# A dense layer over token groups of 512 instead of 384, with its weight remainders taken by VectorE

## The chip, the core and the metric

The kernel runs on one core of a Trainium2 chip. The metric is the device time of one execution in microseconds (us). Engines: TensorE (PE; its weight loads are shown apart as PEld), VectorE (DVE), ScalarE (ACT), GpSimd (POOL), and the queue of SyncE (SP), which here issues nearly all transfers.

## What is computed

Three stages follow each other. First, attention for 2 batches of 8 heads, 768 positions and 64 dimensions; a query sees only the keys whose six random sign bits equal its own. Second, a dense layer over the 1536 tokens with fp32 accuracy; third, a layer of eight experts in which each token goes through the expert with the largest gate logit:

```python
h = x @ w_in                      # 1536 x 512 by 512 x 2048
r = np.maximum(h, 0.0)
x2 = (s * (r * r) + b) @ w_out    # 2048 x 512
logits = x2 @ w_gate              # eight experts
e_idx = np.argmax(logits, axis=1)
# per token: gate_w * sigmoid(x2 @ w_output_gate[:, e]) * (relu(x2 @ w1[e]) @ w2[e])
```

Every large product is made of three in a rounded format: a value is split into a rounded part and its remainder, and high x high, high x low and low x high are added up.

## The kernel before, in words

The order of the work on every engine is the order of the program (a manual schedule); engines wait for each other through semaphores only.

**Attention** runs in 107 calls of `tick` (L230), one tile of 128 queries each. Every sixth tick ends one head pair's half of a batch: 384 tokens are copied to `xs` (L273), GpSimd rounds them to `xh` (L274), and VectorE takes the remainder `xl` in the next tick (L278). These are the dense layer's input, in four groups of 384 tokens, so that each half fills one group (L270). Ticks 84 to 95 are interleaved with the first three weight conversions (`convs`, L1021), and ticks 96 to 106 with the first dense steps.

**The dense layer** (`moe1`, L914) has 64 steps, 16 blocks of 128 hidden units for each of 4 groups, and two more that drain. Step s issues, in this order: the load of a later weight block (`stage`, L328, only in group 0, SP's queue, into five `stg` buffers), `mm1` of step s (L358: 12 matmuls of 384 columns into one PSUM bank, L368), the elementwise work of step s - 1, and `mm2` of step s - 2 (L394: for each of three token tiles three matmuls of 512 columns, L406 to L408). The elementwise work for s < 14 is four ScalarE operations (Relu L375, Square L379, scale and bias L380, rounding L381 to `gh`) and one on VectorE, the remainder `gl` (L390); from step 14 on, ScalarE L375, VectorE L383, ScalarE L384, VectorE L392. `r`, `gh` and `gl` have two buffers each.

**The weight conversion** (`conv`, L340) in steps 0 to 12 prepares block s + 3, once, in group 0: the weights arrive as 64 bit numbers, and VectorE puts the 32 bit ones together with three integer operations for each of two halves (L347, L349, L353). ScalarE rounds each half (L354), and GpSimd takes the remainder (L355):

```python
for k in range(2):
    nc.vector.scalar_tensor_tensor(m[k], t[k][:, :, 0], 29, m[k], ...)      # L353
    nc.scalar.copy(w[:, k, 0, :], m[k].bitcast(F32))                        # L354
    nc.gpsimd.tensor_tensor(w[:, k, 1, :], m[k].bitcast(F32), ...)          # L355
    yield
```

VectorE's order in such a step is: 2 x L347, 2 x L349, 2 x L353, then `gl` of the step before. The converted block of step s is first read by `mm1` three steps later.

**The gates** (`gate`, L410) follow each group: the three result tiles `y` are copied to `x2` (L416, ScalarE but for one), transposed on TensorE (`flip`, L429), multiplied with the gate weights (`logits`, L422), and VectorE finds each token's expert and weight in a row of small operations; then `x2` is stored to DRAM (L498). A gate is a generator: it is advanced once per step, and three times per step from step 50 on, after `mm1`, after the elementwise work and after `mm2`. `x2` and the transposed tiles share the five `stg` buffers. After the third gate `route_early` (L522) picks two experts with at least 128 tokens among those gated so far, loads their weights into the buffers of weight blocks that are done (L595) and gathers 128 tokens for each (L606), so that the first two of twelve expert passes can run while the last gate and `route` (L610) work. `mark` (L517) writes the table `am`, and `route` allots a table `pb` (L657), both in `stg` buffers.

**The expert layer** (`moe2`, L822) runs twelve passes of 128 tokens: per pass four weight segments, each split into two tiles by ScalarE (L752) and VectorE (L754), 12 matmuls per segment, and transposes of the hidden tile (`th`, L770) into three rotating `ht` buffers, two of which lie where the last group's `xh` and `xl` were. More passes follow only if the counts need them (`extra`, L883).

Of the kernel before, what the change touches and what calls it, by code (L numbers as in the profile page):

```python
# [20 lines left out]
NP = H // 2  # L21
# [5 lines left out]
XW = 513  # L27
NKEEP, NCONST = 222, 840
# [8 lines left out]
class Kernel:  # L37
# [5 lines left out]
    def consts(self, pool):  # L43
# [13 lines left out]
        self.cw = bf("cwb", 128)  # L57
# [172 lines left out]
    def tick(self, t):  # L230
# [35 lines left out]
        if t >= 15 and (t - 15) % 6 == 0:  # L266
            u = (t - 15) // 6
            n, half = divmod(u, 2)
            b, p = divmod(n, NP)
            g = 2 * b + half  # L270
            xp = st["xp"].pop(u)
            xs = self.xs_p.tile([128, HS], F32, name="xs")
            nc.scalar.copy(xs, xp)  # L273
            nc.gpsimd.tensor_scalar(self.xh[g][:, p, :], xs, 1.0, 1.0, ALU.mult, ALU.mult)  # L274
            st["xl"] = (self.xl[g][:, p, :], xs, self.xh[g][:, p, :].bitcast(F32))
        elif "xl" in st:
            o, i0, i1 = st.pop("xl")
            nc.vector.tensor_tensor(o, i0, i1, ALU.subtract)  # L278
# [61 lines left out]
    def conv(self, j):  # L340
# [11 lines left out]
        for k in range(2):  # L352
            nc.vector.scalar_tensor_tensor(m[k], t[k][:, :, 0], 29, m[k], ALU.logical_shift_right, ALU.bitwise_or)  # L353
            nc.scalar.copy(w[:, k, 0, :], m[k].bitcast(F32))  # L354
            nc.gpsimd.tensor_tensor(w[:, k, 1, :], m[k].bitcast(F32), w[:, k, 0, :].bitcast(F32), ALU.subtract)  # L355
            yield

    def mm1(self, s):  # L358
# [5 lines left out]
        h = self.ps1.tile([128, HS], F32, tag=tag, name="h", bufs=2 if tag == "tp" else 1)  # L364
# [7 lines left out]
    def elem(self, s):  # L372
        nc = self.nc
        r = self.g_p.tile([128, HS], F32, name="r", bufs=2)
        nc.scalar.activation(r, self.h.pop(s), AF.Relu)  # L375
        gh = self.g_p.tile([128, HS], F32R, name="gh", bufs=2)
        gl = self.g_p.tile([128, HS], F32R, name="gl", bufs=2)
# [16 lines left out]
    def mm2(self, s):  # L394
# [6 lines left out]
        for tt in range(3):  # L401
# [8 lines left out]
    def gate(self, g):  # L410
        nc, v = self.nc, self.nc.vector
        last = g == 3
        xts = []
        for tt in range(3):
# [4 lines left out]
        lts = self.cv_p.tile([128, 3, 128], F32, tag="cvm", name="lts", bufs=4)  # L419
        xt = []  # L420

        def logits(ts):  # L422
            lt = self.ps1.tile([128, 3, 128], F32, tag="tp", name="lt", bufs=2)
# [5 lines left out]
        def flip(tt):  # L429
            bank = ("pv", 1) if last and tt == 2 else ("tp", 2)  # L430
# [5 lines left out]
            else:  # L436
                if tt == 0:
                    self.t3 = self.x3_p.tile([128, 3, 4, 128], F32, tag="xl3", name="xt3")
                t = self.t3[:, tt]
            (nc.scalar.copy if last and tt == 1 else v.tensor_copy)(t, tp)  # L440
            xt.append(t)

        if last:
            for tt in range(3):
                flip(tt)
            yield
            logits([0, 1, 2])
# [5 lines left out]
        lp = self.ps1.tile([128, 3, 2 * E], F32, tag="tp", name="lp", bufs=2)  # L453
        for tt in range(3):
            nc.tensor.matmul(lp[:, tt, :], lts[:, tt, :], self.sel, start=True, stop=True)
        lg = self.small("lg", 3, 2 * E)
# [3 lines left out]
        bc = lambda a, k: a.unsqueeze(2).to_broadcast([128, 3, k])  # L460
        mx = self.small("mx", 3)
        v.tensor_reduce(mx, lg[:, :, 0:E], AX.X, ALU.max)
        df = self.small("df", 3, E)
        v.tensor_tensor(df, lg[:, :, 0:E], bc(mx, E), ALU.subtract)
        ex = self.small("ex", 3, E)
# [3 lines left out]
        wv = self.small("wv", 3, E)  # L469
        desc = self.c[:, 188:196].unsqueeze(1).to_broadcast([128, 3, E])  # L470
        v.scalar_tensor_tensor(wv, df, 0.0, desc, ALU.is_equal, ALU.mult)
        mw = self.small("mw", 3)
        v.tensor_reduce(mw, wv, AX.X, ALU.max)
        oh = self.oh[:, 3 * g:3 * g + 3, 0:E]
        v.tensor_tensor(oh, wv, bc(mw, E), ALU.is_equal)
        if not last:
            for k in range(3 * g, 3 * g + 3):
                v.tensor_tensor(self.cum[:, k + 1, :], self.cum[:, k, :], self.oh[:, k, 0:E], ALU.add)
            yield
        po = self.small("df", 3, E)  # L480
        v.tensor_tensor(po, oh, lg[:, :, E:2 * E], ALU.mult)
        ov = self.small("ov", 3)
        v.tensor_reduce(ov, po, AX.X, ALU.add)
        eo = self.small("eo", 3)
# [3 lines left out]
        se = self.small("se", 3)  # L488
# [3 lines left out]
        sc = self.small("sc", 3)  # L492
        v.reciprocal(sc, se)
        for tt in range(3):
            x2 = xts[tt]
            v.tensor_copy(x2[:, 512:513], sc[:, tt:tt + 1])
            k = 3 * g + tt
# [24 lines left out]
    def route_early(self):  # L522
        v, pe = self.nc.vector, self.nc.tensor
        nt = 9
        ps = self.ps1.tile([128, nt + 1, E], F32, tag="tp", name="rps", bufs=2)
        pe.matmul(ps, self.ones, self.hc.unsqueeze(2).to_broadcast([128, nt + 1, E]), start=True, stop=False)
        pe.matmul(ps, self.ones, self.cum, start=False, stop=False)
# [7 lines left out]
        for t in range(0, nt, 3):  # L535
            self.mark(t, t + 3, r[:, t:t + 3])
# [30 lines left out]
        pc = self.small("pe", 9, E)  # L567
# [29 lines left out]
        for P in range(2):  # L597
            self.gather(P, TOK - 384)
# [11 lines left out]
    def route(self):  # L610
        v, pe = self.nc.vector, self.nc.tensor
        oh = self.oh
        ps = self.ps1.tile([128, 4, E], F32, tag="tp", name="rps", bufs=2)
        pe.matmul(ps, self.ones, self.hc[:, 6:10].unsqueeze(2).to_broadcast([128, 4, E]), start=True, stop=False)
        pe.matmul(ps, self.ones, self.cum[:, 9:10, :].to_broadcast([128, 4, E]), start=False, stop=False)
        pe.matmul(ps[:, 0:3, :], self.tri, oh[:, 9:12, 0:E], start=False, stop=False)
        for t in range(3):
            pe.matmul(ps[:, t + 1:4, :], self.ones, oh[:, 9 + t:10 + t, 0:E].to_broadcast([128, 3 - t, E]), start=False, stop=(t == 2))
        n = ps[:, 3, :]
        sl = self.small("sl", E)  # L620
        v.tensor_scalar(sl, n, 1.0 / 128, MAGIC, ALU.mult, ALU.add)
        mr = self.small("pe", 9, E)[:, 0:3, :]
        v.tensor_tensor(mr, oh[:, 9:12, 0:E], ps[:, 0:3, :], ALU.mult)
        v.tensor_scalar(sl, sl, MAGIC, None, ALU.subtract)
        r = self.small("rr", 9)[:, 0:3]
# [3 lines left out]
        q = self.small("rq", 9)[:, 0:3]  # L629
# [9 lines left out]
        v.tensor_copy(oh[:, 9:12, E], q)  # L639
# [12 lines left out]
        self.mark(9, NT, r)  # L652
# [117 lines left out]
    def th(self, P, n):  # L770
# [5 lines left out]
        pool, tag = ((self.x3_p, "xh3"), (self.x3_p, "xl3"), (self.m2_p, "ht"))[self.nht % 3]  # L776
# [340 lines left out]
```

## Time and profile before

| | |
|---|---|
| median of 3 runs | 729.1 us (728.49 to 730.5) |
| profiled execution, its own time | 730.24 us |
| its span, first to last instruction | 728.5 us |
| TensorE busy | 687.6 us (94%) |
| VectorE busy | 490.1 us (67%) |
| ScalarE busy | 435.3 us (60%) |
| GpSimd busy | 242.8 us (33%) |
| mean granted TensorE clock | 0.984 of full speed |

Times in the rows are us from the span's start, durations us unless marked ns. A timeline row has start, duration, engine, line, operation, output <- inputs, shape, how many were merged, and in brackets the idle time of that engine just before with what ended it. Merged rows span from the first start to the last end. Consecutive matmuls overlap in the rows (one of L368 lasts 0.34 us, the next starts 0.18 later), so what one costs in a stream is the distance of the starts.

### The profile page before, as it was taken

The page shows a single profiled execution, that of the slowest core. Times are in us where ns is not written, and L with a number is a line of the kernel's source. Part 1 is how long each engine was busy: PE and PEld are TensorE (multiplying, and loading weights), DVE is VectorE, ACT ScalarE, POOL GpSimd, SP SyncE. Part 2 cuts the span into 40 slices and gives each one's busy share as a digit, 9 for nine tenths or more (in the row PEclk, how much of TensorE's full clock was granted, in tenths as well). Part 3 has the DMA queues.
Part 4 walks back from the last instruction along what each step waited for, and adds up shares of the span by engine and source line. Part 5 has one row for each costly group of instructions (what it writes and reads, how often), then busy time and mean ns, then how long its engine had stood idle before and what let it go on. Part 6 is the DMA issues. An engine that isn't in the chain of part 4 may idle for free. (4 is left out here: it accounts for less than half of the span.)

```text
span 728.5 us, 10938 instructions
## 1 busy us (share of the span) xinstructions
PE 687.6 (94%) x3888; PEld 537.1 (74%) x3888; DVE 490.1 (67%) x916; ACT 435.3 (60%) x802; POOL 242.8 (33%) x239
## 2 busy tenths in 40 slices
PE   6799999999998997779999999999999899999995
PEld 3566666666665666669889988988997668888873
DVE  4677768767779799992334233325557999898960
ACT  4788878878886574664222322232246599888850
POOL 4566667666667566450000000000100023212111
PEclk7899999999999999999999999999999999999999
DMA  9941352332503255500001000101660162111680
GB/s 207 230 88 66 87 146 72 87 110 55 199 1 105 70 190 215 173 30 1 0 1 45 1 1 0 44 1 41 237 258 1 49 244 98 44 45 44 213 315 28
DMA packets 17581, 69.94 MB, mean 96 GB/s; under 512 B 2990, under 2 KB 3886, under 8 KB 14064
## 3 DMA queue, kind: packets, MB, share of 16 engines
q1 hardware_dynamic: 15472, 62.61, 27.5%
q0 software_dynamic: 2048, 6.56, 2.7%
q8 instruction: 33, 0.54, 0.3%
q14 instruction: 28, 0.23, 0.1%
HBM read 100.61 MB, written 6.43 MB: 147 GB/s over the span
## 5 line engine op out<-in xcount | busy, mean ns | idle before, releaser
L368 PE MATMUL h<-xh,w 128*128 128x384 f32 x512 | 143.8, 341 | 0.0
L257 DVE TENSOR_REDUCE nm<-sp 128x1 f32<-128x768 f32 x96 | 91.4, 952 | 43.9 <-PE sp L255 41.9
L754 DVE TENSOR_TENSOR ring<-raw,ring 128x1024 fp32r<-128x1024 f32 x96 | 113.3, 1220 | 11.1 <-ACT ring L752 10.6
L308 POOL TENSOR_SCALAR pe<-pe,rd 128x768 f32<-128x768 f32 x96 | 90.5, 943 | 65.6 <-DVE rd L307 51.3
L368 PEld LDWEIGHTS h<-xh,w 128*128 128x128 f32 x512 | 93.8, 188 | 5.7 <-issue 2.2
L752 ACT CAST ring<-raw 128x1024 fp32r<-128x1024 f32 x96 | 96.4, 1056 | 2.3 <-issue 2.3
L384 ACT ACTIVATE gh<-r,sb 128x384 fp32r<-128x384 f32 x50 | 30.9, 617 | 105.7 <-DVE r L383 72.3
L312 ACT ACTIVATE pe<-sp,nm 128x768 f32<-128x768 f32 x96 | 88.0, 916 | 7.3 <-DVE rd L265 5.1
L291 PE MATMUL tp<-consts,pe 128*128 128x128 f32 x576 | 82.6, 281 | 6.0 <-POOL pe L308 3.9
L407 PE MATMUL y<-w,gl 128*128 128x512 f32 x192 | 76.3, 397 | 12.7 <-DVE gl L390 12.6
L368 PE MATMUL h<-xl,w 128*128 128x384 f32 x256 | 86.3, 337 | 0.0
L291 PEld LDWEIGHTS tp<-consts,pe 128*128 128x128 f32 x576 | 66.0, 143 | 20.7 <-issue 10.7
L254 PE MATMUL sp<-ka,qa 128*128 128x384 f32 x192 | 75.8, 395 | 4.6 <-ACT pe L312 2.6
L406 PE MATMUL y<-w,gh 128*128 128x512 f32 x192 | 75.6, 394 | 0.0
L408 PE MATMUL y<-w,gh 128*128 128x512 f32 x192 | 75.0, 391 | 0.0
L322 PE MATMUL xp<-pt,v 128*64 128x384 f32 x384 | 73.7, 506 | 0.0
L606 POOL DMA_INDIRECT xg<-x2d,ix x2 | 2.1, 1064 | 193.8 <-DVE r L383 193.5
L255 PE MATMUL sp<-kb,qb 128*128 128x384 f32 x192 | 66.4, 346 | 0.0
L392 DVE SCALAR_TENSOR_TENSOR gl<-r,sb,gh 128x384 fp32r<-128x384 f32 x50 | 31.0, 619 | 52.4 <-ACT gh L384 52.4
L295 ACT COPY pt<-tp 128x384 f32<-128x384 f32 x96 | 46.1, 480 | 33.2 <-PE tp L291 32.9
L254 PEld LDWEIGHTS sp<-ka,qa 128*128 128x128 f32 x192 | 37.5, 195 | 34.3 <-ACT pt L299 12.6
L355 POOL TENSOR_TENSOR w<-cvm,w 128x512 fp32r<-128x512 f32 x32 | 48.8, 1545 | 34.6 <-ACT w L354 34.4
(229 smaller groups left out, 1268.0 us busy)
## 6 DMA issues: line engine op xcount, KB each, us to landing
raw<-w SPq DMA_DIRECT2D x56, 1024.0 KB
stg<-wio SPq DMA_DIRECT2D x28, 512.0 KB
d<-qk SPq DMA_DIRECT2D x14, 768.0 KB
dz<-qz SPq DMA_DIRECT2D x14, 384.0 KB
x2d<-x SPq DMA_DIRECT2D x12, 256.5 KB
v<-v SPq DMA_DIRECT2D x8, 384.0 KB
tmp<-wio SPq DMA_DIRECT2D x4, 512.0 KB
d<-qk SPq DMA_DIRECT2D x4, 384.0 KB
```

Source lines behind the costliest of these rows:

```text
L254: nc.tensor.matmul(sp[:, m, 0:HS], QA[h][:, q], KA[h][:, k], start=True, stop=False)
L257: nc.vector.tensor_reduce(nm, sp[:, :, 0:HS], AX.XY, ALU.max, negate=True)
L291: nc.tensor.transpose(tp[:, kt, :], pe3[:, (3 * j + kt) * 128:(3 * j + kt + 1) * 128], self.ident)
L308: nc.gpsimd.tensor_scalar(pe, pe, rd, 1.0, ALU.mult, ALU.mult)
L312: nc.scalar.activation(pe.rearrange("p (n k) -> p n k", n=2), sp[:, :, 0:HS], AF.Exp, bias=nm, accum_out=den)
L322: nc.tensor.matmul(xp[64 * h:64 * h + 64, :], v[:, h, kt, :], st["pt"][2 * u + h][:, kt, :], start=(kt == 0), stop=(kt == KT - 1))
L368: nc.tensor.matmul(h, a, b, start=(n == 0), stop=(n == 11))
L406: nc.tensor.matmul(y, gh[:, c], w[:, 0], start=(j == 0), stop=False)
L407: nc.tensor.matmul(y, gl[:, c], w[:, 0], start=False, stop=False)
L408: nc.tensor.matmul(y, gh[:, c], w[:, 1], start=False, stop=(j == 15))
L752: nc.scalar.copy(t[:, 0], src)
L754: nc.vector.tensor_tensor(t[:, 1], src, t[:, 0].bitcast(F32), ALU.subtract)
```

## The change

The dense layer takes three groups of 512 tokens (`GW`, `NG`; `GT` = 4 token tiles each, `NE` = 8 tiles known to `route_early`). There are 48 steps and two that drain; `mm1` has 512 columns, `mm2` four token tiles and the elementwise tiles 512 columns; `r` has one buffer instead of two. Where a half of 384 tokens crosses a group border, `xh` and `xl` are written in two pieces. In `conv` both halves are assembled and rounded first, and then VectorE takes both remainders. In each gate four `y` tiles are copied, in turns by ScalarE and VectorE; in the first two gates the logits of a tile and the transposes of the next are issued in one piece. The `ht` buffers become four slots in two tiles. A constant (`cw`) lies in another pool. Step numbers tied to the end of the layer move with it.

```diff
+GW = 512
+NG = TOK // GW
+GT = GW // 128
+NE = 12 - GT
...
-            nc.gpsimd.tensor_scalar(self.xh[g][:, p, :], xs, 1.0, 1.0, ALU.mult, ALU.mult)
-            st["xl"] = (self.xl[g][:, p, :], xs, self.xh[g][:, p, :].bitcast(F32))
+            st["xl"] = []
+            t0 = b * S + half * HS
+            lo = t0
+            while lo < t0 + HS:
+                g, c = divmod(lo, GW)
+                hi = min((g + 1) * GW, t0 + HS)
+                xh, xl = self.xh[g][:, p, c:c + hi - lo], self.xl[g][:, p, c:c + hi - lo]
+                src = xs[:, lo - t0:hi - t0]
+                nc.gpsimd.tensor_scalar(xh, src, 1.0, 1.0, ALU.mult, ALU.mult)
+                st["xl"].append((xl, src, xh.bitcast(F32)))
+                lo = hi
...
             nc.scalar.copy(w[:, k, 0, :], m[k].bitcast(F32))
-            nc.gpsimd.tensor_tensor(w[:, k, 1, :], m[k].bitcast(F32), w[:, k, 0, :].bitcast(F32), ALU.subtract)
+        for k in range(2):
+            nc.vector.tensor_tensor(w[:, k, 1, :], m[k].bitcast(F32), w[:, k, 0, :].bitcast(F32), ALU.subtract)
             yield
...
-        h = self.ps1.tile([128, HS], F32, tag=tag, name="h", bufs=2 if tag == "tp" else 1)
+        h = self.ps1.tile([128, GW], F32, tag=tag, name="h", bufs=2 if tag == "tp" else 1)
...
-        r = self.g_p.tile([128, HS], F32, name="r", bufs=2)
+        r = self.g_p.tile([128, GW], F32, name="r", bufs=1)
...
-        for tt in range(3):
+        for tt in range(GT):
...
-            (v.tensor_copy if last and tt == 1 else nc.scalar.copy)(x2[:, 0:512], self.y[g][tt])
+            (v.tensor_copy if tt % 2 else nc.scalar.copy)(x2[:, 0:512], self.y[g][tt])
...
-            bank = ("pv", 1) if last and tt == 2 else ("tp", 2)
+            bank = ("pv", 1) if last and tt == 2 else ("prep", 1) if last and tt == 3 else ("tp", 2)
...
-            (nc.scalar.copy if last and tt == 1 else v.tensor_copy)(t, tp)
+            (nc.scalar.copy if last and tt % 2 else v.tensor_copy)(t, tp)
...
-            for f in (lambda: flip(0), lambda: flip(1), lambda: logits([0]), lambda: flip(2), lambda: logits([1]), lambda: logits([2])):
-                f()
+            flip(0)
+            yield
+            for tt in range(1, GT):
+                logits([tt - 1])
+                flip(tt)
                 yield
+            logits([GT - 1])
+            yield
...
-        nt = 9
+        nt = NE
...
-            self.gather(P, TOK - 384)
+            self.gather(P, TOK - GW)
...
-        pool, tag = ((self.x3_p, "xh3"), (self.x3_p, "xl3"), (self.m2_p, "ht"))[self.nht % 3]
+        half, slot = divmod(self.nht % 4, 2)
+        if self.nht in (0, 2):
+            self.hts.append(self.x3_p.tile([128, 2, 2, 4, 128], F32R, tag=("xh3", "xl3")[half], name="ht"))
...
-        for s in range(64 + 2):
+        ns = 16 * NG
+        for s in range(ns + 2):
...
-            if s > 49:
+            if s > ns - 15:
                 next(gates, None)
...
-                if s == (60, 61, 63, 64)[k]:
+                if s == ns + (-4, -3, -1, 0)[k]:
```

## Rows read from the trace of the kernel before

**Rows 1.** The page's part 2: TensorE's busy tenths and granted clock, 40 slices.

```profile
PE   6799999999998997779999999999999899999995
...
PEclk7899999999999999999999999999999999999999
```

**Rows 2.** Busy time by stretch: stretch, length, PE, PEld, DVE, ACT, POOL, clock, DMA share, GB/s.

```profile
252.03:337.24 85.21, 72.65 (x359) 59.15 (x358) 76.31 (x99) 48.93 (x89) 42.88 (x29) 1.00 0.37 130
337.24:553.79 216.55, 216.38 (x1170) 192.48 (x1169) 88.42 (x211) 66.14 (x121) 2.13 (x2) 1.00 0.14 53
...
600.00:690.00 90.00, 90.00 (x439) 74.25 (x438) 83.58 (x84) 80.02 (x104) 20.93 (x14) 1.00 0.26 85
```

**Rows 3.** Timeline of TensorE: step 5 begins; one whole step of group 2.

```profile
276.30 0.34 PE L368 MATMUL h<-xh,w 128*128 128x384 f32 x1
...
395.01 0.34 PE L368 MATMUL h<-xh,w 128*128 128x384 f32 x1
...
397.13 0.39 PE L406 MATMUL y<-w,gh 128*128 128x512 f32 x1
...
399.18 0.34 PE L368 MATMUL h<-xh,w 128*128 128x384 f32 x1
```

**Rows 4.** Timeline of VectorE: one step of group 0 and the next one's beginning.

```profile
286.58 2.95 DVE L347 TENSOR_SCALAR cvm<-stg 128x512 int32<-128x512 int32 x2
289.45 1.28 DVE L349 SCALAR_TENSOR_TENSOR cvm<-stg,cvm 128x512 int32<-128x512 int32 x2
290.65 1.28 DVE L353 SCALAR_TENSOR_TENSOR cvm<-stg,cvm 128x512 int32<-128x512 int32 x2
291.86 0.54 DVE L390 TENSOR_TENSOR gl<-r,gh 128x384 fp32r<-128x384 f32 x1
292.33 2.96 DVE L347 TENSOR_SCALAR cvm<-tmp 128x512 int32<-128x512 int32 x2
```

**Rows 5.** Timelines of VectorE (first) and GpSimd: L347 and L355 in group 0.

```profile
252.79 0.75 DVE L347 TENSOR_SCALAR cvm<-stg 128x512 int32<-128x512 int32 x2
...
256.08 2.72 POOL L355 TENSOR_TENSOR w<-cvm,w 128x512 fp32r<-128x512 f32 x2 [3.95 <-ACT w L354]
...
286.31 2.93 POOL L355 TENSOR_TENSOR w<-cvm,w 128x512 fp32r<-128x512 f32 x2 [3.15 <-ACT w L354]
```

**Rows 6.** Timelines of ScalarE (three rows) and TensorE in the same step.

```profile
286.74 0.49 ACT L375 ACTIVATE r<-h 128x384 f32<-128x384 f32 x1
...
288.56 0.51 ACT L381 CAST gh<-r 128x384 fp32r<-128x384 f32 x1
291.42 1.17 ACT L354 CAST w<-cvm 128x512 fp32r<-128x512 f32 x2 [2.34 <-DVE cvm L353]
...
292.46 0.50 PE L407 MATMUL y<-w,gl 128*128 128x512 f32 x1 [1.31 <-DVE gl L390]
```

**Rows 7.** Groups by form: count | busy us, mean ns | idle us before, releasers.

```profile
L754 DVE TENSOR_TENSOR ring<-raw,ring 128x1024 fp32r<-128x1024 f32 x96 | 113.3, 1220 | 11.1 <-ACT ring L752 10.6
...
L375 ACT ACTIVATE r<-h 128x384 f32<-128x384 f32 x64 | 31.2, 488 | 34.7 <-PE h L368 34.6
...
L390 DVE TENSOR_TENSOR gl<-r,gh 128x384 fp32r<-128x384 f32 x14 | 7.7, 547 | 4.1 <-ACT gh L381 4.1
...
L416 ACT COPY x<-y 128x512 f32<-128x512 f32 x11 | 6.5, 588 | 8.4 <-PE y L408 7.9
```

**Rows 8.** Timelines of VectorE and GpSimd in the last ticks of attention.

```profile
241.82 1.64 DVE L353 SCALAR_TENSOR_TENSOR cvm<-stg,cvm 128x512 int32<-128x512 int32 x1
...
241.62 1.29 POOL L355 TENSOR_TENSOR w<-cvm,w 128x512 fp32r<-128x512 f32 x1
```

**Rows 9.** Timelines of TensorE and VectorE: transposes in the third gate and their first copy.

```profile
488.19 1.04 PE L433 MATMUL xtp<-consts,x 128*128 128x128 f32 x8
...
488.82 0.69 DVE L440 COPY xt<-xtp 128x512 f32<-128x512 f32 x1 [5.44 <-PE xtp L433]
```

**Rows 10.** Timeline of TensorE: the products of the routing table.

```profile
575.90 0.46 PE L680 MATMUL ips<-bm,am 128*128 128x40 bf16 x12 [2.23 <-DVE ht L781]
```

**Rows 11.** The tile x2d: gathers from it, issue to landing.

```profile
DMA to landing us min/median/max: 3.4/4.1/8.1
```

More of the change, by code (lines that the diff above doesn't have):

```diff
@@ L411, in gate @@
         nc, v = self.nc, self.nc.vector
-        last = g == 3
+        last = g == NG - 1
         xts = []
-        for tt in range(3):
+        for tt in range(GT):
             x2 = self.stg_p.tile([128, XW], F32, tag="stg", name="x2")
-            (v.tensor_copy if last and tt == 1 else nc.scalar.copy)(x2[:, 0:512], self.y[g][tt])
+            (v.tensor_copy if tt % 2 else nc.scalar.copy)(x2[:, 0:512], self.y[g][tt])
             xts.append(x2)
         yield
-        lts = self.cv_p.tile([128, 3, 128], F32, tag="cvm", name="lts", bufs=4)
+        lts = self.cv_p.tile([128, GT, 128], F32, tag="cvm", name="lts", bufs=4)
         xt = []
         def logits(ts):
-            lt = self.ps1.tile([128, 3, 128], F32, tag="tp", name="lt", bufs=2)
+            lt = self.ps1.tile([128, GT, 128], F32, tag="tp", name="lt", bufs=2)
             for ti in ts:
@@ L487, in gate @@
         nc.scalar.activation(eo, ov, AF.Exp, scale=-1.0)
-        se = self.small("se", 3)
+        se = self.small("se", GT)
         v.tensor_reduce(se, ex, AX.X, ALU.add)
@@ L491, in gate @@
         v.scalar_tensor_tensor(se, eo, 1.0, se, ALU.add, ALU.mult)
-        sc = self.small("sc", 3)
+        sc = self.small("sc", GT)
         v.reciprocal(sc, se)
-        for tt in range(3):
+        for tt in range(GT):
             x2 = xts[tt]
             v.tensor_copy(x2[:, 512:513], sc[:, tt:tt + 1])
-            k = 3 * g + tt
+            k = GT * g + tt
             nc.sync.dma_start(out=self.x2d[k * 128:k * 128 + 128, :], in_=x2)
@@ L523, in route_early @@
         v, pe = self.nc.vector, self.nc.tensor
-        nt = 9
+        nt = NE
         ps = self.ps1.tile([128, nt + 1, E], F32, tag="tp", name="rps", bufs=2)
-        pe.matmul(ps, self.ones, self.hc.unsqueeze(2).to_broadcast([128, nt + 1, E]), start=True, stop=False)
-        pe.matmul(ps, self.ones, self.cum, start=False, stop=False)
+        pe.matmul(ps, self.ones, self.hc[:, 9 - nt:10].unsqueeze(2).to_broadcast([128, nt + 1, E]), start=True, stop=False)
+        pe.matmul(ps, self.ones, self.cum[:, 0:nt + 1], start=False, stop=False)
         pe.matmul(ps[:, 0:nt, :], self.tri, self.oh[:, 0:nt, 0:E], start=False, stop=True)
@@ L534, in route_early @@
         yield
-        for t in range(0, nt, 3):
-            self.mark(t, t + 3, r[:, t:t + 3])
+        for t in range(0, nt, GT):
+            self.mark(t, t + GT, r[:, t:t + GT])
             yield
@@ L612, in route @@
         oh = self.oh
[L613 to L619, printed above, removed]
+        ps = self.ps1.tile([128, GT + 1, E], F32, tag="tp", name="rps", bufs=2)
+        pe.matmul(ps, self.ones, self.hc[:, 9 - GT:10].unsqueeze(2).to_broadcast([128, GT + 1, E]), start=True, stop=False)
+        pe.matmul(ps, self.ones, self.cum[:, NE:NE + 1, :].to_broadcast([128, GT + 1, E]), start=False, stop=False)
+        pe.matmul(ps[:, 0:GT, :], self.tri, oh[:, NE:12, 0:E], start=False, stop=False)
+        for t in range(GT):
+            pe.matmul(ps[:, t + 1:GT + 1, :], self.ones, oh[:, NE + t:NE + 1 + t, 0:E].to_broadcast([128, GT - t, E]), start=False, stop=(t == GT - 1))
+        n = ps[:, GT, :]
         sl = self.small("sl", E)
         v.tensor_scalar(sl, n, 1.0 / 128, MAGIC, ALU.mult, ALU.add)
-        mr = self.small("pe", 9, E)[:, 0:3, :]
-        v.tensor_tensor(mr, oh[:, 9:12, 0:E], ps[:, 0:3, :], ALU.mult)
+        mr = self.small("pe", 9, E)[:, 0:GT, :]
+        v.tensor_tensor(mr, oh[:, NE:12, 0:E], ps[:, 0:GT, :], ALU.mult)
         v.tensor_scalar(sl, sl, MAGIC, None, ALU.subtract)
-        r = self.small("rr", 9)[:, 0:3]
+        r = self.small("rr", 9)[:, 0:GT]
         v.tensor_reduce(r, mr, AX.X, ALU.add)
@@ L628, in route @@
         v.scalar_tensor_tensor(tn, sl, -128.0, n, ALU.mult, ALU.add)
-        q = self.small("rq", 9)[:, 0:3]
+        q = self.small("rq", 9)[:, 0:GT]
         v.tensor_scalar(q, r, 1.0 / 128, MAGIC, ALU.mult, ALU.add)
@@ L651, in route @@
         v.tensor_reduce(p9, px, AX.X, ALU.add)
-        self.mark(9, NT, r)
+        self.mark(NE, NT, r)
         T = p9[:, E:E + 1]
@@ L967, in attention @@
         self.xh, self.xl = {}, {}
-        for g in range(4):
-            p = self.x3_p if g == 3 else self.x_p
-            self.xh[g] = p.tile([128, NP, HS], F32R, name=f"xh{g}")
-            self.xl[g] = p.tile([128, NP, HS], F32R, name=f"xl{g}")
+        for g in range(NG):
+            p, k = (self.x3_p, 3) if g == NG - 1 else (self.x_p, g)
+            self.xh[g] = p.tile([128, NP, GW], F32R, name=f"xh{k}")
+            self.xl[g] = p.tile([128, NP, GW], F32R, name=f"xl{k}")
+        self.cw = self.bit_p.tile([128, 128], BF16, name="cwb", bufs=1)
         st = self.st = dict(preps={0: []}, pe={}, pt={}, xp={}, v={}, z={}, load={})
```

68 lines of the change are left out of this document (33 added, 35 removed).

## The prediction

> **What bounds the kernel now.** I read the page's busy slices first: TensorE is at 9 tenths almost everywhere except at the start and the end and in slices 16 to 18 (273 to 328 us), and its granted clock is at full speed there, so the level is 2.4 GHz and idle time, not the clock, is to be looked for [rows 1]. Second, the table by stretches, cut at the dense layer's group borders. Its first group lasts 85.21 us with TensorE busy for 72.65; the other three, with the drain of the last, last 216.55 us with TensorE busy for 216.38; the expert layer from 600 to 690 us is TensorE without a gap [rows 2]. So there are two bounds: in group 0 something else, afterwards TensorE's own instructions.
>
> Third, the timeline of one undisturbed step. The 12 matmuls of the first product (384 columns) take 395.01 to 397.13, 2.12 us or 0.177 each; the 9 of the second (512 columns) take 397.13 to 399.18, 2.05 us or 0.227 each [rows 3]. A column costs 0.460 ns in the narrow form and 0.444 in the wide one: each matmul brings a part that doesn't grow with its columns.
>
> Fourth, the timeline of a step of group 0. VectorE's conversion repeats from 286.58 to 292.33, 5.75 us, without a gap [rows 4], and TensorE stands 1.31 us before L407, released by VectorE's gl of L390 [rows 6]. Of the 5.75 us the two L347 take 2.95; at 252.79, with GpSimd idle for 3.95 us until 256.08, the same two took 0.75. The slow pair lies at 286.58 to 289.53, GpSimd's two L355 at 286.31 to 289.24 [rows 5]. So the conversion is held up by GpSimd's remainders beside it, not by VectorE's own work alone.
>
> **The change part by part.**
> *Dense layer, TensorE.* 64 steps of 12 + 9 matmuls become 48 of 12 + 12. The second product keeps 576 matmuls. The first goes from 768 of 384 columns to 576 of 512: 768 x 0.177 = 135.7 us against 576 x 0.227 = 130.8, 5 us less. I take 0.227 for the wide form from rows of the same shape [rows 3]. A plain proportion to the columns would give 0.236 and no gain, which is one bound; the row decides. The Trainium skill, page "TensorE: Matmul & The Clock Gate", section "Back-to-back issue gap", gives for isolated matmuls at full clock the columns over 2.4 GHz plus 2.5 ns. By that rule 768 x 162.5 ns against 576 x 215.8 ns would leave 0.5 us and the sum would end 4.5 us later, which speaks against this change. The trace disagrees: 177 ns at 384 columns.
>
> *Group 0, VectorE.* GpSimd's L355 goes away and two subtractions of 128x512 come to VectorE. From 0.547 us at 384 (L390, mean) and 1.22 at 1024 columns [rows 7] one takes 0.68, and 0.61 start to start, as the pairs of L349 and L353 show (1.28 for two). With GpSimd idle L347 falls to 0.75 [rows 5]. A step becomes 0.7 + 1.2 + 1.2 + 1.2 + 0.61 (gl at 512) = 4.9 us, plus waits. The loop that counts is longer, as r has one buffer: Relu waits for the gl before it. ScalarE's four operations take 286.74 to 289.07, 2.33 us [rows 6], and 0.1 more each at 512 (0.488 against 0.588 [rows 7]): 2.75. Then the first L354 0.62, two subtractions 1.22, gl 0.68 and two handovers between engines of 0.09 (the first L353 ends near 291.33, L354 starts at 291.42 [rows 4, 6]): 5.45 us. TensorE's new step is 24 x 0.227 = 5.45. They are equal as far as I can read it, and the second product reads gl a whole step after it is made, so a lag of up to one step is free. I cost this at nothing: TensorE covers it, and if the cover goes, each 0.1 us over 5.45 costs 1.3 us in 13 steps.
>
> *Group 0, sum.* Steps 0 to 4 (252.03 to 276.30 [rows 2, 3]) hold 24.27 us, of which 5 x 2.12 + 3 x 2.05 = 16.8 is the dense layer, so 7.5 us is TensorE's rest of attention, which stays. New: 16 first products and 14 second ones, 360 x 0.227 = 81.7, plus 7.5: 89.2 us against 85.21. The group is 4 us longer but holds 512 tokens.
>
> *Groups 1 and 2.* Before, 48 first and 50 second products are 48 x 2.12 + 50 x 2.05 = 204.3 of the 216.55, so gates and small work on TensorE cost 12.3 us over nine token tiles. Now eight tiles: 10.9. The second gate, called three times a step, puts the logits of tile 0 and of tile 3 straight behind their own transposes; TensorE then waits for the copy: transposes start 488.19, the copy runs 488.82 to 489.51 [rows 9], against TensorE free at about 488.55, so 1.0 us, twice. Sum: 32 + 34 products x 12 x 0.227 = 179.8, + 10.9 + 2.0 + 0.4 for the last wait on gl = 193.1. The dense layer is 282.3 instead of 301.76 us: 19.5 less.
>
> *End of attention.* The first three conversions lie in ticks 84 to 95, where VectorE is the busy engine. Six subtractions add 6 x 0.61 = 3.7 us; the second L353 of each conversion, stretched to 1.64 beside L355 [rows 8], falls to about 0.65, up to 3 us back. I take +1.0, nearest to the difference, between -2 (the relief alone, the subtractions in idle time) and +3.7. The split of xs at group borders gives 8 more operations to VectorE and to GpSimd; they lie under TensorE's matmuls and are in these bounds.
>
> *Tail.* The last gate has four tiles. VectorE gets a copy of y (0.68), wider logits and marks (0.3) and some longer small ones: 1.2 us, in the chain for which TensorE already waits 2.23 us at 575.90 [rows 10]. TensorE's 0.7 us of transposes and logits disappear in that wait. +1.2, between 0 and +4.
>
> *At nothing:* four ht slots instead of three (TensorE has no gap from 600 to 690); the weight loads for the experts, issued as many steps before the end as now, in longer steps; the twelve x2d stores in three lots of four; the constant cw in another pool; the y copies shared with VectorE, beside a first product of 2.7 us.
>
> **Sum.** 19.5 - 1.0 - 1.2 = 17.3 us. The profiled execution takes 730.24 us (span 728.5 and 1.74 around it), so 712.9; the median shown is 1.14 below that execution: 711.8.
>
> **Rivals.**
> 1. *The conversion still paces group 0.* If the loop is 5.8 us (longer handovers, stg loads late), 13 x 0.35 = 4.6 us more with no slack counted, about 716. For: the two loops are equal. Against: one step of slack, which would swallow it. Chance 0.10.
> 2. *No saving per matmul.* 0.236 for the first product: 576 x 0.009 = 5 us more, 717. For: the first product keeps another operand order than the second. Against: in the trace the narrow form costs more per column. Chance 0.03. The Trainium skill's rule from the same page and section points this way.
> 3. *A buffer wait at the gates.* Of the five stg buffers four now hold x2 until its store has landed, so am (second gate) and pb (last) take one of these; VectorE would stand before them in order. Landings of the x2d gathers take 3.4 to 8.1 us [rows 11]; at the second gate a step of slack hides most, in the tail 4 us show: 716. Against: VectorE's route work and its splits stand between the stores and pb. Chance 0.05.
> 4. *L347 stays slow.* If its 1.5 us come from something other than L355 (the landing weights, say), VectorE's step is today's 5.75 plus 1.22 for the subtractions, 0.14 for the wider gl and some 0.2 of waiting on L354: 7.3 us. Thirteen of these end at 252.8 + 1.0 + 95 = 349; with what follows (2.5 us of a second product, one step of 5.45) group 1 begins at 357 instead of 342: 727, no change, and 733 with the costly ends of attention and tail. It decides from a step over about 6.1 us on, a pair of 1.7. For: 1.5 us is what most L347 take. Against: 0.75 at 252.79 [rows 5]. Chance 0.06.
> 5. *Slower: an expert pass more.* The two early passes take 128 tokens each of two experts that have 128 among the tokens gated by then: 1152 so far, 1024 now. If an expert falls below 128, its early tile is part empty and a thirteenth pass is entered at the end, which runs alone: gather 4 us [rows 11], eight splits of 1.22 [rows 7], 48 matmuls of 0.227 and an estimated 5 us of transposes, copies and store: 30 us, 742. It decides at a count of 128. Against: the reference's inputs (seed 0) send 167 and 856 of the first 1024 tokens to two experts. Chance 0.03.
> That GpSimd keeps the remainders can't be: the diff names VectorE in their only place.
>
> **The numbers.** Forecast 0.73, rivals 0.10, 0.03, 0.05, 0.06 and 0.03. The forecast's own bounds: attention at -2 (3.0 less), tail at 0 (1.2 less) and no waits in the second gate (2.0 less) make 705.6; attention at +3.7 and tail at +4 make 717.3. Rivals 1 to 3 reach 717 too. The range is 706 to 718; it leaves out rivals 4 and 5 and a little on either side. A measurement here can tell about 0.3%, 2.2 us, from no change. Faster 0.91: the forecast and rivals 1 to 3. Same 0.04, two thirds of rival 4; slower 0.05, the rest of it and rival 5.
>
> **What would show it.** Right: first products of 2.7 us; steps of 5.45 us; L347 pairs near 0.75 in group 0 and no wait of L407 on gl there; TensorE's first dense matmul at 252 to 254 us and the dense layer's end at about 535; a wait of about 1 us before logits twice in the second gate. Wrong: L347 still at 1.5 us, steps of group 0 above 5.6, gaps in the expert layer, or VectorE standing before mark or pb for a DMA.

## The result and the profile after

The changed kernel takes 716.58 us (median of 4 runs, 715.79 to 717.34) against 729.33 us: the ratio is 0.9824, 95% interval 0.9805 to 0.9843, 1.8% faster. The profiled execution takes 717.34 us, its span 715.6.

The page of the kernel after, part 1 and TensorE's tenths of part 2, beside [rows 1]:

```profile
PE 685.9 (96%) x3696; PEld 512.4 (72%) x3696; DVE 479.4 (67%) x913; ACT 429.3 (60%) x764; POOL 198.5 (28%) x215
...
PE   6799999999998899999999999999999899999995
```

The dip of slices 16 to 18 is gone. Busy time by stretch, kernel after, cut at the first dense matmul, the first of group 1 and the first of the expert layer; the third row lies within the expert layer (columns as in [rows 2]):

```profile
253.80:344.33 90.53, 90.53 (x401) 70.12 (x400) 70.09 (x126) 55.19 (x89) 1.93 (x4) 1.00 0.34 123
344.33:539.29 194.96, 193.40 (x921) 155.20 (x919) 78.84 (x167) 53.69 (x84) 2.13 (x2) 1.00 0.15 57
590.00:680.00 90.00, 90.00 (x435) 73.51 (x434) 82.96 (x82) 78.76 (x102) 20.85 (x14) 1.00 0.25 81
```

The dense layer lasts 90.53 + 194.96 = 285.49 us in place of 301.76. TensorE's busy time in it falls from 289.03 [rows 2] to 283.93 and its idle time from 12.73 to 1.56: the 12.56 us of waits in group 0 are gone, and 1.56 us of waits are new, in the second gate. So 11.2 of the 16.3 us are waits. The first dense matmul is 1.77 us later (253.80 against 252.03), and what follows the dense layer lasts 715.6 - 539.29 = 176.31 against 174.71 us, 1.6 more. From 590 to 680 us, in the expert layer, TensorE has no gap, as before.

Timeline of TensorE, kernel after, one undisturbed step of group 1, beside [rows 3]:

```profile
410.05 0.40 PE L380 MATMUL h<-xh,w 128*128 128x512 f32 x1
...
412.85 0.39 PE L418 MATMUL y<-w,gh 128*128 128x512 f32 x1
...
413.55 0.39 PE L418 MATMUL y<-w,gh 128*128 128x512 f32 x1
...
415.58 0.40 PE L380 MATMUL h<-xh,w 128*128 128x512 f32 x1
```

The second product takes 2.73 us, 0.2275 per matmul. The first takes 2.80, 0.2333: the price that the forecast had wrong. Steps are 5.54 us, not 5.45. The border is not sharp: the first three matmuls of the second product still take 0.70 us (412.85 to 413.55, 0.233 each), the other nine 2.03, 0.226 each.

Timeline of VectorE, kernel after, one step of group 0, beside [rows 4]:

```profile
299.60 0.76 DVE L358 TENSOR_SCALAR cvm<-stg 128x512 int32<-128x512 int32 x2
300.27 1.29 DVE L360 SCALAR_TENSOR_TENSOR cvm<-stg,cvm 128x512 int32<-128x512 int32 x2
301.48 1.29 DVE L364 SCALAR_TENSOR_TENSOR cvm<-stg,cvm 128x512 int32<-128x512 int32 x2
303.12 1.29 DVE L367 TENSOR_TENSOR w<-cvm,w 128x512 fp32r<-128x512 f32 x2 [0.36 <-ACT w L365]
304.33 0.69 DVE L402 TENSOR_TENSOR gl<-r,gh 128x512 fp32r<-128x512 f32 x1
304.94 0.76 DVE L358 TENSOR_SCALAR cvm<-stg 128x512 int32<-128x512 int32 x2
```

The first pair (L347 before) takes 0.76 us in place of 2.95, and the loop 5.34, under TensorE's 5.54. TensorE has no idle time in group 0 (90.53 of 90.53 us busy).

### The profile page after: what moved, and what is told of

It reads as the page before. It is cut to its first block, busy times and chain, and to the rows that moved or that the text cites. A ratio compares the mean times of both kernels' runs of the same rounds, so it can differ in the third digit from the quotient of the medians.

```text
span 715.6 us, 10439 instructions
## 1 busy us (share of the span) xinstructions
PE 685.9 (96%) x3696; PEld 512.4 (72%) x3696; DVE 479.4 (67%) x913; ACT 429.3 (60%) x764; POOL 198.5 (28%) x215
## 5 line engine op out<-in xcount | busy, mean ns | idle before, releaser
L380 PE MATMUL h<-xh,w 128*128 128x512 f32 x384 | 130.0, 400 | 0.0
L319 POOL TENSOR_SCALAR pe<-pe,rd 128x768 f32<-128x768 f32 x96 | 92.2, 961 | 70.5 <-DVE rd L318 52.5
L380 PEld LDWEIGHTS h<-xh,w 128*128 128x128 f32 x384 | 72.2, 188 | 19.0 <-issue 1.4
L380 PE MATMUL h<-xl,w 128*128 128x512 f32 x192 | 76.0, 396 | 0.0
L396 ACT ACTIVATE gh<-r,sb 128x512 fp32r<-128x512 f32 x34 | 24.6, 725 | 85.2 <-PE y L420 43.0
L387 ACT ACTIVATE r<-h 128x512 f32<-128x512 f32 x48 | 28.7, 598 | 61.7 <-PE h L380 37.0
L404 DVE SCALAR_TENSOR_TENSOR gl<-r,sb,gh 128x512 fp32r<-128x512 f32 x34 | 25.6, 752 | 53.9 <-ACT gh L396 53.9
```

The lines of the kernel that those rows point to most:

```text
L319: nc.gpsimd.tensor_scalar(pe, pe, rd, 1.0, ALU.mult, ALU.mult)
L380: nc.tensor.matmul(h, a, b, start=(n == 0), stop=(n == 11))
```

## Experiments

**The two halves of the change, one by one.** conv_alone is the kernel before with the conversion's part:

```diff
-            nc.gpsimd.tensor_tensor(w[:, k, 1, :], m[k]...)
+        for k in range(2):
+            nc.vector.tensor_tensor(w[:, k, 1, :], m[k]...)
```

> The kernel before (four groups of 384) with one part of the change alone: VectorE takes both remainders, GpSimd none. Theory (the two slow L347 come from GpSimd's remainders beside them): the pair of L347 falls from 2.95 to about 0.75 us in group 0, VectorE's step there goes from 5.75 to 0.7 + 3 x 1.2 + 0.55 = 4.9 us, TensorE needs only 4.17, so 13 steps give back about 11 us, the end of attention takes 1 to 2 of them again: 719 to 721 us. Rival (L347 is slow for another reason, such as landing weights): the step is 5.75 + 1.22 = 7 us, and the time goes to about 745.

Measured 723.95 us (721.75 to 724.69), ratio 0.9918 (0.9906 to 0.9930). Busy time of conv_alone in group 0, and the timeline of VectorE there:

```profile
252.81:329.45 76.64, 72.16 (x359) 59.35 (x358) 67.85 (x125) 49.08 (x89) 1.34 (x3) 1.00 0.40 145
```

```profile
294.39 0.76 DVE L347 TENSOR_SCALAR cvm<-stg 128x512 int32<-128x512 int32 x2
295.06 1.29 DVE L349 SCALAR_TENSOR_TENSOR cvm<-stg,cvm 128x512 int32<-128x512 int32 x2
296.27 1.29 DVE L353 SCALAR_TENSOR_TENSOR cvm<-stg,cvm 128x512 int32<-128x512 int32 x2
297.64 1.29 DVE L356 TENSOR_TENSOR w<-cvm,w 128x512 fp32r<-128x512 f32 x2
298.85 0.55 DVE L391 TENSOR_TENSOR gl<-r,gh 128x384 fp32r<-128x384 f32 x1
299.32 0.76 DVE L347 TENSOR_SCALAR cvm<-stg 128x512 int32<-128x512 int32 x2
```

The mechanism is as said: no remainder on GpSimd, no slow pair, a step of 4.93 us. The size is smaller than expected: group 0 lasts 76.64 us against 85.21, 8.6 less and not 11, since only eight steps (281.59 to 321.13) run at the conversion's pace; in the others TensorE has enough work of its own. The median gains 5.9 us; the profiled run, 721.96, is at the low end of the spread.

groups_alone is the kernel after with the remainders on GpSimd, that diff the other way round.

> The kernel after (three groups of 512) with the remainders back on GpSimd. Theory: the pair of L358 is 2.95 us again, VectorE's step in group 0 becomes 2.95 + 1.25 + 1.2 + 0.65 = 6.05 us against 5.54 on TensorE, 13 x 0.5 less about one step's slack = 3 to 6 us slower in group 0, and 0 to 1.8 us faster at the end of attention: 718 to 722 us. Rival (with 512 tokens per step the conversion is hidden either way, so that the move of the remainders is worth nothing): 715 to 717 us.

Measured 715.05 us, ratio 0.9801 (0.9789 to 0.9814): the rival, at its lower end. Busy time by stretch in groups_alone, cut at the same places:

```profile
251.60:342.17 90.57, 90.57 (x402) 70.10 (x400) 77.69 (x100) 56.36 (x89) 48.28 (x30) 1.00 0.34 123
342.17:537.12 194.95, 193.38 (x920) 155.15 (x919) 78.81 (x167) 53.77 (x84) 2.13 (x2) 1.00 0.15 57
```

Timeline of VectorE in groups_alone:

```profile
298.77 2.96 DVE L358 TENSOR_SCALAR cvm<-stg 128x512 int32<-128x512 int32 x2
...
304.66 2.96 DVE L358 TENSOR_SCALAR cvm<-stg 128x512 int32<-128x512 int32 x2
...
327.62 0.68 DVE L401 TENSOR_TENSOR gl<-r,gh 128x512 fp32r<-128x512 f32 x1
```

Timeline of TensorE in groups_alone, the first matmul that reads this gl:

```profile
328.55 0.39 PE L418 MATMUL y<-w,gl 128*128 128x512 f32 x1
```

The pair is 2.96 us again and VectorE's step 5.89, 0.35 longer than TensorE's. Yet group 0 lasts 90.57 us with TensorE busy for all of it, because gl has up to a step to spare. That slack is nearly used up: the time from the end of a gl to the first matmul that reads it shrinks by 0.35 us a step, from 2.00 to 0.25 in the last six slow steps (328.55 - 328.30 in the rows; 4.39 there in the kernel after). So with 512 tokens per step the move of the remainders hides nothing that wasn't hidden, but one more slow step at this rate would have used the slack up. What the move does change is the start of the dense layer, 251.60 in place of 253.80; the next experiment asks how much of that is its doing.

**The end of attention.** first3_pool is the kernel after with this in `conv`:

```diff
+            if j < 3:
+                nc.gpsimd.tensor_tensor(w[:, k, 1, :], m[k]...)
+                yield
-        for k in range(2):
+        for k in range(2) if j >= 3 else ():
             nc.vector.tensor_tensor(w[:, k, 1, :], m[k]...)
```

> The kernel after, where GpSimd takes the remainders of the first three conversions (in the last ticks of attention), as before the change, and VectorE the other thirteen. Theory: the six subtractions on VectorE are what made the first dense matmul 1.77 us later (253.80 instead of 252.03); it comes at 252.0 to 252.5 and the time is 1.3 to 1.8 us less, about 715. Rival: the later start is the eight more pieces of the split input; the first dense matmul stays at 253.5 to 254 and the time at 716.6.

Measured 715.29 us, ratio 0.9797 (0.9784 to 0.9811). Timeline of TensorE, the first dense matmul, in first3_pool:

```profile
252.04 0.48 PE L383 MATMUL h<-xh,w 128*128 128x512 f32 x1
```

The start comes where the theory had it. But 1.77 us is the difference of two starts, and only a part of it lies where the remainders are taken. Busy time by stretch, from the first score matmul of tick 84, where the conversions begin, to the first dense matmul, in the kernel before, the kernel after and first3_pool (columns as in [rows 2]):

```profile
215.33:252.03 36.70, 32.47 (x191) 21.09 (x190) 32.84 (x66) 25.84 (x59) 25.42 (x23) 0.95 0.25 86
216.36:253.80 37.44, 32.30 (x192) 21.39 (x190) 33.18 (x73) 26.15 (x59) 19.75 (x18) 0.95 0.24 85
215.89:252.04 36.15, 31.55 (x191) 20.30 (x190) 32.31 (x67) 25.80 (x59) 26.05 (x24) 1.00 0.25 88
```

In the five kernels with three groups and the first three conversions on GpSimd (groups_alone, first3_pool and the later gate2_gp, gate2_first3 and aligned) this stretch takes 36.15 to 36.17 us at a granted clock of 1.00. In the seven with VectorE it takes 37.44 to 38.94 at 0.91 to 0.95. So the move costs 1.29 us in the traces (37.44 against 36.15), as in the medians (716.58 against 715.29): TensorE idles 5.14 us in place of 4.60 and is busy 0.75 longer, with its clock at the lower level, 1.2 GHz, from 227.84 to 231.25, just after it had waited 1.19 us for ScalarE at 227.39. The kernel before has such a fall too, from 233.44 to 236.85, after a wait of 1.40 us at 231.97. The edit puts back two things, the engine and the order: in the kernel after both halves are assembled in one call, and in two of the three conversions VectorE then waits 0.20 us for ScalarE's rounding. Which of the two costs more was not tried.

The other 1.03 us of the 1.77 are there before the first conversion (216.36 against 215.33). Of these, 0.57 are there at tick 24 (71.40 against 70.83), where eleven kernels with the same attention lie anywhere from 70.30 to 71.40: they differ in no instruction up to there. The other 0.46 come in ticks 24 to 84, which take 144.9 to 145.4 us in every kernel with three groups and 144.4 to 144.5 in the two with four. The pieces of the split `xs` are the new work there and the likely reason, not shown by a run of its own.

**The second gate.** Timeline of TensorE in the kernel after, the waits of the second gate:

```profile
453.01 0.43 PE L438 MATMUL lt<-xt,wg 128*32 128x128 f32 x8 [0.78 <-DVE xt L452]
...
462.26 0.43 PE L438 MATMUL lt<-xt,wg 128*32 128x128 f32 x8 [0.78 <-DVE xt L452]
```

These are the logits of tiles 0 and 3, behind their own transposes. late_gate skips one call ahead of each:

```diff
             flip(0)
             yield
+            if g == NG - 2:
+                yield
             for tt in range(1, GT):
...
+            if g == NG - 2:
+                yield
             logits([GT - 1])
```

> The kernel after, where the second gate skips one of its three calls per step ahead of the first logits and one ahead of the last, so that the logits of tile 0 and of tile 3 no longer follow their own transposes directly. Theory: two waits of about 1 us on TensorE go, steps 34 and 35 (8.66 and 8.79 us) lose 2 us together, 714.6 us. Rival: the early routing comes one step (5.5 us) later and its gathers miss the first expert pass: TensorE waits there, 717 to 721 us. Second rival: the transposes' waits only move to the next buffer: 716.6 us.

Measured 716.51 us, ratio 0.9814 (0.9801 to 0.9827): no more than the intervals can tell, because one of the two waits only moved. Timeline of TensorE in late_gate, its one wait there:

```profile
461.67 0.43 PE L438 MATMUL lt<-xt,wg 128*32 128x128 f32 x8 [0.78 <-DVE xt L452]
```

It is now the logits of tile 2, since the calls after `mm1` and after the elementwise work have no other TensorE work between them. From the first to the last dense step it is 0.84 us shorter (273.57 against 274.41). The profiled run had begun that layer 1.2 us later, after a longer fall of the clock in late attention (0.50 of full speed from 234.82 to 241.65). gate2_gp leaves out the right calls, on top of groups_alone, and gate2_first3 does so on top of first3_pool:

```diff
             for tt in range(1, GT):
+                if g == NG - 2 and tt % 2:
+                    yield
                 logits([tt - 1])
...
             logits([GT - 1])
             yield
+            if g == NG - 2:
+                yield
```

> Three groups of 512, all remainders on GpSimd as before the change, and the second gate spread so that no logits follow their own transposes directly (three calls skipped). Theory: 715.05 us of groups_alone less the two waits of 0.78 us and what follows them on TensorE, 1.6 to 2.0 us: 713.0 to 713.6. Rival (late_gate removed one wait and won 0.1 us of 716.6: such waits are taken back later, at the routing): 714.8 to 715.3.

> Three groups of 512, remainders on GpSimd for the first three conversions and on VectorE for thirteen, and the second gate spread as in gate2_gp. Theory: 715.3 us of first3_pool less 1.6 to 2.0: 713.3 to 713.8, and within 0.5 us of gate2_gp, since in group 0 both are hidden by TensorE's 5.54 us per step. Rival (the shorter conversion of VectorE helps once the waits are gone): 1 us or more below gate2_gp.

Measured 713.47 us, ratio 0.9779 (0.9766 to 0.9793), and 713.85, 0.9777 (0.9764 to 0.9790). Busy time by stretch in gate2_gp:

```profile
251.53:342.07 90.54, 90.54 (x401) 70.11 (x400) 78.70 (x100) 56.57 (x89) 44.93 (x30) 1.00 0.34 123
342.07:535.38 193.31, 193.31 (x920) 154.97 (x919) 79.00 (x167) 53.77 (x84) 2.14 (x2) 1.00 0.15 58
```

No idle time is left, and the two groups are 1.64 us shorter than in groups_alone. The early routing a step later costs nothing that shows. The two kernels agree: who takes the remainders from the fourth conversion on doesn't matter here.

**Why the first product costs 0.233.** First the order and the bank, both on the kernel after; kinds:

```diff
-        for kd in range(4):
-            for a, b in ((w[:, 0, kd], xh[:, kd]), (w[:, 0, kd], xl[:, kd]), (w[:, 1, kd], xh[:, kd])):
-                nc.tensor.matmul(h, a, b, ...)
+        for wi, x in ((0, xh), (0, xl), (1, xh)):
+            for kd in range(4):
+                nc.tensor.matmul(h, w[:, wi, kd], x[:, kd], ...)
```

> The kernel after with the 12 matmuls of a first product ordered by kind (four of high x high, four of high weights x low input, four of low weights x high input) in place of three kinds for each of four blocks. First product now 2.80 us (0.233 each), second 2.73 (0.2275). Theory P (twelve accumulations into one bank in a row cost 0.233, whatever the operands): unchanged, 0.233, 716 to 717 us. Rival O (the order of the operands, the same stationary tile twice in a row, makes it 0.233): another price, 0.227 at best, 48 x 12 x 0.006 = 3.5 us less, 713 us.

inter makes `mm2` a generator that stops ahead of each tile, and `mm1` advances it after every three matmuls (cut; the loop over the steps changes with it):

```diff
         for kd in range(4):
             for a, b in (...):
                 nc.tensor.matmul(h, a, b, ...)
+            next(other, None)
...
```

> The kernel after, where in steps 24 to 31 and 40 to 47 the first and the second product are interleaved in threes (three matmuls into h, three into a tile of y, and so on), same matmuls. Theory P (many accumulations into one bank in a row): all 24 matmuls of such a step take 0.227 to 0.229, the step 5.46 to 5.50 instead of 5.54 us, 1 us less in all, 715.5 us. Rival O (the operands of the first product): its matmuls keep 0.233, the step 5.54, 716.6 us. A third, that the first matmuls after a change of bank are the slow ones: above 5.54.

Measured 717.34 us (0.9837, 0.9824 to 0.9849) and 717.23 (0.9830, 0.9817 to 0.9842). Timelines of TensorE, a step of kinds and then two rounds of six in inter:

```profile
409.56 1.09 PE L380 MATMUL h<-xh,w 128*128 128x512 f32 x4
...
412.36 0.39 PE L418 MATMUL y<-w,gh 128*128 128x512 f32 x1
...
415.10 1.09 PE L380 MATMUL h<-xh,w 128*128 128x512 f32 x4
```

```profile
406.26 0.40 PE L380 MATMUL h<-xh,w 128*128 128x512 f32 x1
...
406.96 0.40 PE L420 MATMUL y<-w,gh 128*128 128x512 f32 x1
...
407.65 0.40 PE L380 MATMUL h<-xh,w 128*128 128x512 f32 x1
```

Again 2.80 and 2.74 us; and 1.39 for six, 0.231 each, the mean of the two prices. Neither the order nor the bank sets it. Then the operands. mm1_moving_w and mm2_moving_x each change one moving tile, mm1_stat_x both tiles of the first product:

```diff
# mm1_moving_w
-        xh, xl = self.xh[g], self.xl[g]
+        xh, xl = ([self.w[j][:, 1, t]] * 4 for t in range(2))
...
# mm1_stat_x
-            for a, b in ((w[:, 0, kd], xh[:, kd]), ...
+            for a, b in ((xh[:, kd, 0:128], self.w[j][:, 1, 0]), ...
# mm2_moving_x
-            nc.tensor.matmul(y, gh[:, c], w[:, 0], ...)
+            nc.tensor.matmul(y, gh[:, c], self.xh[g][:, tt], ...)
```

> The kernel after, where the first product's moving tile is a block of the second weights (512 columns, the one that the second product reads) in place of xh and xl; stationary tiles and banks unchanged; the result is another one, so that only the dense layer's steps are read. First product now 0.233 us per matmul, step 5.54. Theory M (the place or kind of the moving tile sets the price): 0.227, step 5.45. Rival S (stationary tile) or B (the bank of h, the position in the step): 0.233, 5.54.

> The kernel after, where the first product has both operands of another kind: 128 columns of xh or xl stationary, a block of the second weights moving, as the second product has them; the bank of h and the order of the steps unchanged; the result is another one, so that only the dense layer's steps are read. Theories M and S (an operand sets the price): 0.227, step 5.45. Rival B (the bank of h or the position in the step): 0.233, step 5.54.

> The kernel after, where the second product's moving tile is xh or xl (512 tokens) in place of the second weights; stationary tiles and banks unchanged; the result is another one, so that only the dense layer's steps are read. Theory M (the place or kind of the moving tile sets the price): the second product's matmuls go from 0.2275 to 0.233 or more, the step from 5.54 to 5.6 us. Rivals S and B: 0.2275 and 5.54 as now.

Timelines of TensorE, a step of mm1_moving_w, one of mm2_moving_x and one of mm1_stat_x (the times of the whole kernels, 712.57, 760.15 and 717.56 us, say nothing, as the routing gets other values):

```profile
407.74 2.88 PE L380 MATMUL h<-w 128*128 128x512 f32 x12
410.46 0.39 PE L418 MATMUL y<-w,gh 128*128 128x512 f32 x1
...
413.18 1.07 PE L380 MATMUL h<-w 128*128 128x512 f32 x4
```

```profile
406.25 0.40 PE L380 MATMUL h<-xh,w 128*128 128x512 f32 x1
...
409.06 0.39 PE L418 MATMUL y<-xh,gh 128*128 128x512 f32 x1
...
411.88 0.40 PE L380 MATMUL h<-xh,w 128*128 128x512 f32 x1
```

```profile
409.95 0.39 PE L380 MATMUL h<-w,xh 128*128 128x512 f32 x1
...
412.74 0.40 PE L418 MATMUL y<-w,gh 128*128 128x512 f32 x1
...
415.51 0.39 PE L380 MATMUL h<-w,xh 128*128 128x512 f32 x1
```

Without xh and xl both products take 2.72 us, 0.227 each. With them in both, 2.81 and 2.82, 0.234 to 0.235. In mm1_stat_x they are the stationary tiles, and the first product takes 2.79 us, 0.2325 each: they are slow in that place too, so that theory M as it was put is too narrow. Its second product, with tiles and order unchanged, takes 2.77 in place of 2.73. So the price goes with reading xh and xl, but not only in the matmuls that read them: neighbours pay as well, as the first three of the second product do in the kernel after.

aligned asks whether it is where they begin:

```diff
+            ent(sb("pad", 1, "right")).tile([128, 8], F32, name="pad")
             self.x3_p = ent(sb("x3", 1, "right"))
```

> gate2_gp plus one unused tile of 32 bytes per partition ahead of the tiles that lie at the far end of the SBUF, so that all of these start on multiples of 64 bytes, as the converted weights and gh and gl already do; no instruction changes. So far xh and xl (and in the expert layer xth, ht and part of the ring) start 32 bytes off such a multiple, the weights on it; in the kernel before, both were 32 bytes off, and its second product cost 0.227. Theory A (a matmul of 512 columns costs 0.234 instead of 0.227 when its stationary and its moving tile lie in different halves of 64 bytes): first product 0.227, step 5.44 to 5.46 instead of 5.54, 46 x 0.09 = 4 us less, and up to 1.2 us in the expert layer: 708.0 to 709.5 us against 713.5. Rival D (the data or kind of xh and xl make them slow, wherever they lie): first product 0.233 to 0.235, step 5.54, 713.5 us.

Measured 711.93 us, ratio 0.9747 (0.9732 to 0.9762). Timeline of TensorE in aligned:

```profile
401.12 0.40 PE L379 MATMUL h<-xh,w 128*128 128x512 f32 x1
...
403.91 0.39 PE L417 MATMUL y<-w,gh 128*128 128x512 f32 x1
...
406.65 0.40 PE L379 MATMUL h<-xh,w 128*128 128x512 f32 x1
```

Theory A falls: 2.79 us and a step of 5.53, 0.01 less and not 0.09. The medians are 1.5 us apart, and so are the profiled runs (711.51 against 713.06). In these, 0.53 us are the dense layer, the shorter steps (283.32 against 283.85), and 0.17 what follows it. The other 0.85 is an earlier first dense matmul (250.68), and 0.72 of that is there at tick 24 (69.58 against 70.30), where starts spread over 1.1 us among kernels that are alike up to there. The unused tile moves tiles of attention too, so part of it may be its doing; that isn't shown. aligned is the fastest version here, 0.8% under the changed kernel (0.9747 / 0.9824).

**What stays open** is why these two tiles are slow to read. A hint, not tried by a run of its own: in the expert layer of the kernel after, the segments whose ring tiles (c % 10 < 2) come from the pool of the stationary tiles have matmuls 0.2293 us apart, the others 0.2335 (means over matmuls 7 to 11 of a segment, 48 and 188 distances of starts), though both read the same kind of weights. That speaks for the place of the two operands against each other and not for the data. In aligned, where all of these tiles start on multiples of 64 bytes, they are 0.2279 and 0.2324, so it isn't the halves of 64 bytes there either. And in the kernel before the same two are 0.2303 and 0.2290. The test would be xh and xl moved by other amounts.

## Why the prediction was right, and where it was off

It forecast 711.8 us, faster, 706 to 718; 716.58 lies inside, near the upper end. Against the profiled execution 712.9 stood against 717.34: 4.4 us, in three terms.

*Dense layer, 282.3 forecast, 285.5 measured.* The step that failed is "I take 0.227 for the wide form from rows of the same shape". The shape was the same, the tiles read were not, and the measured 0.2333 makes 576 x 0.0063 = 3.6 us; that it is more than the 3.2 missing is due to small terms the other way, such as 1.56 us of waits for 2.4. The 5 us that a column's smaller price was to bring shrink to 135.7 - 134.4 = 1.3. So rival 2, no saving per matmul, was nearly the case; its chance of 0.03 was too low, as "the narrow form costs more per column" compared xh and xl with weights. By the rule for isolated matmuls of the Trainium skill, page "TensorE: Matmul & The Clock Gate", section "Back-to-back issue gap", this term was estimated at 0.5 us; the measured 1.3 is nearer to that than to 5, though the rule's 215.8 ns per matmul isn't what the traces show (227 to 235).

*Group 0.* That L347 is slow because of GpSimd's remainders holds, from both sides (conv_alone, groups_alone); so does the loop, 5.34 against 5.45. That it would matter doesn't, at 512 tokens: rival 4 gave the point from which a slow pair decides, a step over 6.1 us. Today's pair with the wider gl is 5.75 + 0.14 = 5.89, under that point, and the text didn't ask what the move was then for. groups_alone measured 5.89 and no wait, with 0.25 us to spare; so rival 1's 5.8 would have cost nothing either.

*Attention's end, +1.0 forecast, +1.77 measured.* From tick 84 on it is 37.44 - 36.70 = +0.74, near the forecast, and the cause is the one named, the conversions' move to VectorE, though 0.75 us of its cost are TensorE's lower clock, which the forecast didn't have. The relief on the other side was real, the L364 pair takes 1.27 us, but smaller than the cost. The remaining 1.03 lie ahead of tick 84: 0.57 within the spread of such starts, which is luck, and 0.46 in ticks 24 to 84, likely the split of xs, which the text put under TensorE's matmuls.

*Second gate, 2.0 forecast.* Two waits, at the tiles named, 0.78 each; taking them away gave 1.64.

*Tail, +1.2 forecast, +1.6 measured.* The size is near, the reason only half of it: up to the routing table's products it is 22.89 us (539.29 to 562.18) against 22.11, and TensorE's wait there is 2.30 against 2.23 [rows 10]; the other 0.8 lies behind. There expert matmuls are a few ns further apart (0.2335 against 0.2290 above): from the table to the 25th of the 48 weight segments it is 62.46 us against 61.99, from there to the start of the last 75.88 against 75.13, and the stretch from its last matmul to the end gives 0.46 back (11.80 against 12.26). Behind its wait for the table the profiled run of the kernel after also shows the lower clock (granted 0.50 from 562.34 to 565.75; none in the kernel before):

```profile
562.00:566.00 4.00, 3.82 (x67) 3.17 (x67) 4.00 (x5) 0.00 (x0) 0.00 (x0) 0.57 0.00 0
```

The first segment then takes 3.86 us in place of 2.67, but a wait of 1.14 us for a gather, which the kernel before has at 584.12, falls away. gate2_gp, whose clock stays up, has such a wait (1.13), and its time after the dense layer, 175.91, is that of groups_alone, whose clock fell (175.92).

Rivals 3 and 5 didn't come: the only other wait of TensorE between the dense layer and the table is 0.39 us, and there are twelve passes as before.

## What to carry to other kernels

A change of two parts has to be costed as three: each alone and both. Here the wider groups alone give the whole gain and some 1.3 us more by the traces (the ratios, 0.9801 against 0.9824, say 1.7, with intervals that overlap), because a longer step on the bounding engine hides the slow conversion, if only just, as well as a faster conversion does. Before work is moved to a fuller engine, compare its loop with the bounding engine's new step plus the slack in its consumers, which is used up step by step. A difference between two starts is read from where the changed work begins, not from the start of the run: here 1.03 of 1.77 us lay ahead of it. And a price per instruction is read from an instruction that reads the same tiles, not only one of the same shape.

## What the runs showed of the hardware that was not expected

Matmuls of one shape, 128x128 by 512 columns, cost 0.227 us in one place and 0.234 in another of the same step, with all operands ready and at the full clock. The 3% go with two of the tiles that are read, as moving and as stationary tile, and reach matmuls beside them that read neither; order and PSUM bank don't matter, and the cause is open.

Moving six subtractions to a busy VectorE lengthened the end of attention by 1.29 us, of which 0.75 are TensorE busy longer, part of the time at 1.2 GHz; none of the five kernels of three groups without the move shows the lower clock there. Behind the wait for the routing table a fall of the clock cost nothing (175.92 us with it, 175.91 without), since a later wait of 1.1 us fell away with it.
